# Two transformer layers on one Trainium2 core: the planner keeps the DMA queue's time, and head outputs wait in a list of their own

## The chip, the cores and the metric

The kernel runs on one core of one Trainium2 (trn2) chip. The core has five engines that run their own instruction streams and wait for one another through semaphores: PE (TensorE, matrix products; its weight loads are shown apart as PEld), ACT (ScalarE), DVE (VectorE), POOL (GpSimd) and SP (SyncE, which here only issues DMA transfers). The metric is the device time of one execution in microseconds. Times of kernels are medians of several runs; a profile shows one execution, with its own time.

## The reference

Input x is 2048 rows of 512 (bf16). Two equal layers follow each other, and both use the same weights:

```
x = x + attention(layernorm(x))     # 32 heads of 16, full softmax over all 2048 keys, then @ wo
x = x + silu(layernorm(x) @ w1) @ w2   # inner width 1792
```

The attention computes `softmax(q @ k.T / 4) @ v` for every head, without a mask. There are 32 x 2048 x 2048 exponentials in each layer.

## The kernel before

**Tiling.** The 2048 rows are cut into four chunks of 512, `c` for the keys and `qc` for the queries, `L` is the layer. Heads come in four groups `g` of eight, and each group in two halves `par` of four heads; the four heads of a half share the 128 rows of PE as four 32-row tiles. One run is (L, qc, g, par) over 16 key tiles `kt`, and in one step of a run one key tile meets 512 queries for four heads, so a run has 16 steps; there are 1024 steps in all. Layer 0's first query chunk goes over the keys in four passes and layer 1's first in two (PASSES), because its keys are only being made then.

**A step.** PE makes four score blocks (`s_ps`, three of them for ACT, and `d_ps`, L763). ACT takes the exponential of three (`p_sb`, L990, in one activation over one block and one over two). DVE and POOL make the fourth by integer arithmetic on the bits of a half-precision number: DVE writes `d_y` (L910), POOL two shifted copies `d_z` (L930), whose sum with weights approximates the exponential; the weights are in scaled copies of V, `VB`, which POOL makes from `VA` (L481). On every second step PE adds up the weighted values of two steps into `o_ps` (L787). The denominators come along as a column of ones in V.

**Everything else is background work**, put between the steps: layer norms (statistics on DVE and POOL, `xn` on DVE at L339, then a DMA transpose on SP into `xnT` or `fT`, L373), projections (`proj_k`, `proj_q`, `proj_v`, all through `mm4`, matmuls at L397), the end of a run (`group_out`: `o_ps` copied to `oT` by DVE, a DMA transpose into `ot` at L499, reciprocal `rec` at L519 and the normalised product into `attn` at L521), the output projection (`out_proj`: four DMA transposes of `attn` into the free part of `wo`, L557, then four products `y_ps` that are added to x, L545) and the feed-forward part (`ffn`: 14 products `h_ps`, tanh on ACT, `hT` on DVE, then `f_ps`). A projected q does not go where it is used at once: DVE copies it to `q` (L442; two buffers), and eight small DMA transfers on SP spread it over `QT` (L444).

**What sets the order.** The order on each engine is fixed when the program is built. Every background job is a generator, whose `yield part(...)` tells what comes next (time on PE, time on DVE, whether it holds the single bank for products, what it needs). `Background` has a queue, a side list for layer norms, and a list of `urgent` ends of runs, each with a step from which it may be taken. A small model of the engines (`Model`) keeps the clocks of PE, ACT and DVE while the program is built; a part is placed into a step when it `fits`, that is when PE would be back in time for ACT, or DVE would end before ACT. Where a step needs something that is not placed yet, `ensure` places it there, fit or not. Where PE has room that no part fills, `fill` places 3 x 4 products with a zero matrix.

**What the model before knows of transfers.** Any part on DVE that does not hold the bank sets `landed` to DVE's clock plus TRANSPOSE = 3.0 (L173), as if a transpose had been issued there; a finished layer norm keeps that number, and what needs it is placed once PE's clock has passed it. SP's own queue is not modelled. The output projection's transposes count as landed at once:

```
            nc.sync.dma_start_transpose(out=aT[:, i, :, :], in_=attn[L, qc][:, i, :])
        bg.done["aT", L, qc] = 0.0
```

The end of a run by DMA is `urgent` from five steps after the run's last one, whether its transpose has landed or not.

Of the kernel before, what the change touches and what calls it, by code (L numbers as in the profile page):

```python
# [23 lines left out]
def part(dve=0.0, pe=0.0, held=False, sums=False, need=None):  # L24

    return Part(held, pe, dve, sums, need)

class Background:

    def __init__(self):  # L30
        self.queue = deque()
        self.side = deque()
        self.urgent = deque()
        self.active = None
        self.done = {None: 0.0}
        self.model = None
# [24 lines left out]
    def advance(self, item):  # L61
        if self.model:
            self.model.charge(item[2])
        try:
            item[2] = next(item[1])
        except StopIteration:
            if item is self.active:
                self.active = None
            else:
                (self.side if self.side and item is self.side[0] else self.queue).remove(item)  # L70
                self.done[item[0]] = self.model.landed if self.model else 0.0

    def heads(self, now):
        return [self.head(now), self.prime(self.side[0]) if self.side else None]

    def fits(self, item):
        if item is None or item[2].need not in self.done:
            return False
        return self.model.fits(item[2], self.done[item[2].need])
# [11 lines left out]
class Model:  # L91
# [8 lines left out]
    FIX = 0.69  # L100
    FROM_ACT = 0.17
    FROM_DVE = 0.06
    TRANSPOSE = 3.0

    def __init__(self, slack, margin):
        self.slack, self.margin = slack, margin
        self.pe = self.act = self.dve = self.ready = self.free = 0.0
        self.s1 = self.sd = self.copied = self.landed = 0.0
        self.s2 = [0.0, 0.0]
        self.mode = None  # L110

# [25 lines left out]
    def pv(self, groups):  # L137
# [2 lines left out]
        self.pe += self.GROUP * groups  # L140
        self.summed = self.pe + self.TO_DVE

    def pe_end(self, pe, sums):
        start = max(self.pe, self.free, self.copied if sums else 0.0)
        return start + pe + self.SWITCH * (self.mode != "B")

    def fits(self, cost, landed=0.0):
        held, pe, dve, sums, _ = cost
        if landed > self.pe:
            return False  # L150
        if pe:
            end = self.pe_end(pe, sums) + self.SWITCH
            return end + self.GROUP + self.TO_ACT + self.margin <= self.act
        if dve:
            return max(self.dve, self.ready if held else 0.0) + dve <= self.act + self.slack
        return True
# [5 lines left out]
    def charge(self, cost):  # L162
        held, pe, dve, sums, _ = cost
        if pe:
            self.pe = self.pe_end(pe, sums)
            self.mode = "B"
            self.ready = self.pe + self.TO_DVE
        elif dve:
            self.dve = max(self.dve, self.ready if held else 0.0) + dve
            if held:  # L170
                self.free = self.dve + self.FROM_DVE
            else:
                self.landed = self.dve + self.TRANSPOSE  # L173
        elif held:
            self.act = max(self.act, self.ready) + self.TANH
            self.ready = self.act + self.FROM_ACT

@with_exitstack
def kernel(
# [10 lines left out]
    nc = tc.nc  # L190
# [59 lines left out]

    x1 = [x1pool.tile([P, 4, D], BF16, name=f"x1_{c}")[:] for c in range(NC)]
    x_sb = {}

    def load_x(c, src=None, parts=1):
        x_sb[c] = xpool.tile([P, 4, D], BF16, name="x", tag="x")
# [31 lines left out]
    bg = Background()  # L287
# [5 lines left out]
    attn = {}  # L293
# [58 lines left out]
    def ln_pair(c, i):  # L352

        stats[c, i] = yield from ln_stats(c, (i, i + 1))
# [11 lines left out]
    def ln_chunk(c, dst):  # L366

        for i in (0, 2):
            mv, rstd = stats.pop((c, i))
            for u in range(2):  # L370
                yield part(0.57)
                xn = ln_apply(c, i + u, mv[:, u, :], rstd[:, u, :])
                nc.sync.dma_start_transpose(out=dst[:, i + u, :, :], in_=xn[:])  # L373

    def ln_ahead(c):
        for i in (0, 2):
# [43 lines left out]
    def proj_q(L, c, g):  # L420


        yield part(need=("ln", L, c))
        q_ps = yield from mm4(
            "q_ps", lambda ct: w_qkv[:, ct, P * g : P * (g + 1)], lambda ct: xnT[L, c][:, :, ct, :]
        )
        if (L, c) == (0, 0):
            QT[g] = qpool.tile([P, 2, 512], BF16, name="QT", tag=f"QT{g}")
            for par in range(2):
                if par == 1 and g == 0:  # L430
                    nc.scalar.activation(
                        QT[g][:, par, :], q_ps, ACT.Copy, scale=masks[par][:, 0:1]
                    )
                    return
                nc.vector.tensor_scalar_mul(
                    out=QT[g][:, par, :], in0=q_ps, scalar1=masks[par][:, 0:1]
                )
                if par == 0 and g > 0:
                    yield part(0.65, held=True)
            return  # L440
        q = qpool.tile([P, 512], BF16, name="q", tag="q", bufs=2)
        nc.vector.tensor_copy(out=q[:], in_=q_ps)  # L442
        for r in range(0, P, 16):
            nc.sync.dma_start(QT[g][r : r + 16, r // 16 % 2, :], q[r : r + 16, :])  # L444

    def new_v(L, c):
        VA[L, c] = vpool.tile([P, 4, VW], BF16, name="VA", tag="VA")
# [44 lines left out]
    def by_dma(L, qc, g, par):  # L492
        return (L, qc) not in PASSES and (L, qc, g, par) != (1, NC - 1, NG - 1, 1)

    def group_out(L, qc, g, par, oT):

        if by_dma(L, qc, g, par):
            ot = opool.tile([P, 4, P], BF16, name="ot", tag="ot")
            nc.sync.dma_start_transpose(out=ot[:], in_=oT[0])  # L499
            yield part(0.25)  # L500
            att = ot[:].rearrange("p t (j s) -> p t j s", j=4)
        else:
            at_once = 4 if len(oT) <= 2 else 2
            yield part(pe=0.06 * at_once * len(oT), sums=True)
            att = bank("att").rearrange("p (t j s) -> p t j s", t=4, j=4)
            for tq in range(4):
                if tq == at_once:
                    yield part(pe=0.06 * at_once * len(oT), held=True)
                for i, o in enumerate(oT):
                    nc.tensor.matmul(  # L510
                        att[:, tq, :, :].rearrange("p j s -> p (j s)"),
                        lhsT=o[:, tq * P : (tq + 1) * P],
                        rhs=ident[:, :],
                        start=(i == 0),
                        stop=(i == len(oT) - 1),
                    )
            yield part(0.25, held=True)
        rec = small.tile([P, 4, 4, 1], FP32, name="rec", tag="rec")
        nc.vector.reciprocal(rec[:], att[:, :, :, 16:17])  # L519
        yield part(0.43, held=not by_dma(L, qc, g, par))  # L520
        nc.vector.tensor_tensor(  # L521
            out=attn[L, qc][:, :, P * g : P * (g + 1)].rearrange(
                "p t (j s) -> p t j s", s=32
            )[:, :, :, 16 * par : 16 * par + 16],
            in0=att[:, :, :, 0:DH],
            in1=rec[:].to_broadcast([P, 4, 4, DH]),
            op=ALU.mult,
        )
# [23 lines left out]
    def out_proj(L, qc):  # L552
        if (L, qc) == (0, 0):
            load_wo()
        aT = wo[0][:, CT : 2 * CT, :].rearrange("p t (c q) -> p t c q", c=CT)
        for i in range(4):
            nc.sync.dma_start_transpose(out=aT[:, i, :, :], in_=attn[L, qc][:, i, :])  # L557
        bg.done["aT", L, qc] = 0.0
        for i in range(4):
            yield from out_add(qc, i, aT[:, i, :, :])  # L560
            if i % 2:
                bg.add_side(None, ln_pair(qc, i - 1))
        bg.add_side(("fT", L, qc), ln_ffn(L, qc))
# [21 lines left out]
    class W1:  # L585
# [14 lines left out]

        def get(self, ft):
            self.load(ft + 2)
            return self.tiles.pop(ft)

    def ffn(L, c):
# [133 lines left out]
    for ts in pv_steps.values():  # L739
        t, k = ts[0]  # L740
# [148 lines left out]
    def end_run(t, key, o):  # L889

        nc.vector.tensor_copy(out=o, in_=o_tiles[key][:])  # L891
        if not final[key]:
            return
        L, qc, pi, g, par = key
        need = ("aT", *((L, qc - 1) if qc else (L - 1, NC - 1))) if (L, qc) != (0, 0) else None
        gen = end_group(L, qc, g, par)
        if by_dma(L, qc, g, par):
            bg.urgent.append((t + 5, gen, need, next(gen)))
        else:
            bg.urgent.append((t + 2, gen, need, None))  # L900

# [51 lines left out]
    with tc.manual_schedule(  # L953
# [59 lines left out]
        for t in range(1, len(steps)):  # L1013
# [5 lines left out]
            L, qc, pi, g, par, kt, j = a_blks[0]  # L1019
# [37 lines left out]
            if not busy and m.fill_fits(FILL):  # L1057
                n = fill(FILL)
                if n:
                    m.pv(n)  # L1060
        t = len(steps) + 1
# [38 lines left out]
```

## Time and profile before

| | |
|---|---|
| median of 3 runs | 1686.08 us (1683.26 to 1686.69) |
| the profiled execution | 1692.16 us, of which 1690.4 us are the span from the first instruction to the last |
| ACT busy | 1513.3 us, 90% of the span |
| PE busy | 1515.2 us, 90% |
| POOL, DVE busy | 1127.4 us, 67%; 1051.1 us, 62% |
| mean granted clock of PE | 0.950 of full |

A row of the groups reads: line, engine, operation, output <- inputs, shape, count, then busy time and the mean of one in ns, then how long the engine was idle just before them and what ended that. A row of the waits reads: who waited, for whom: total us, times, longest. A row of the stretches gives each engine's busy time in a window, with the number of its instructions that touch the window, then the granted clock of PE (PEclk, 1.00 is full), the mean share of the DMA engines and GB/s.

### The profile page before, as it was taken

The numbers are of one execution on the slowest core, as the hardware profiler recorded it, in microseconds if no ns is written. First come the engines' busy times: TensorE is split into PE (matmuls) and PEld (weight loads), VectorE is DVE, ScalarE is ACT, GpSimd is POOL, SyncE is SP. The second block draws the span as 40 slices with busy tenths as digits, with TensorE's granted clock in tenths as the row PEclk, the third lists the DMA queues.
The fourth block names the chain that finished last, engine by engine and source line by source line (L and its number), as shares of the span: only waits on it lengthen the run. The fifth ranks groups of instructions, "written<-read, shape, count | busy, mean of one in ns | idle before, by whom it ended". The sixth has DMA issues, their size and how long they took to land.

```text
span 1690.4 us, 34407 instructions
## 1 busy us (share of the span) xinstructions
PE 1515.2 (90%) x13471; PEld 468.3 (28%) x13471; DVE 1051.1 (62%) x1723; ACT 1513.3 (90%) x2169; POOL 1127.4 (67%) x1180
## 2 busy tenths in 40 slices
PE   7889997898899988999888979889889898899998
PEld 2222332232222322222222323223222232222323
DVE  4776765666666656666666647666557655576544
ACT  4888997998899988999889959899889998899992
POOL 3677866676776767767766757767667676676750
PEclk7898998999999989999999989999899999999999
DMA  3101012101111011201021010120102101121101
GB/s 118 27 13 26 4 26 54 35 17 44 39 39 28 29 28 42 44 23 34 19 51 38 8 32 11 47 48 13 33 20 48 35 20 30 39 42 26 29 14 47
DMA packets 154770, 55.84 MB, mean 33 GB/s; under 512 B 134896, under 2 KB 154096, under 8 KB 154608
## 3 DMA queue, kind: packets, MB, share of 16 engines
q1 hardware_dynamic: 154608, 53.65, 13.5%
q8 instruction: 105, 1.72, 0.5%
q14 instruction: 57, 0.47, 0.1%
HBM read 28.57 MB, written 4.19 MB: 19 GB/s over the span
## 4 chain that ended last, share of the span: by engine, by line
ACT 66%; PE 21%; DVE 4%; DMA 3%; issue 3%; SPq 2%; POOL 0%; DVEq 0%; ACTq 0%
ACT p_sb L990 62%; PE o_ps L787 7%; PE s_ps L763 6%; ACT t_sb L566 3%; SPq L444 2%; PE k_ps L397 2%; PE v_ps L397 1%; DVE d_y L910 1%; PE y_ps L397 1%; PE q_ps L397 1%; DMA wo<-attn 1%; PE d_ps L763 1%; DMA xnT<-xn 1%; DMA ot<-oT 1%; PE h_ps L397 1%
## 5 line engine op out<-in xcount | busy, mean ns | idle before, releaser
L990 ACT ACTIVATE p_sb<-s_ps 128x512 bf16<-128x512 f32 x2042 | 1489.5, 1075 | 130.0 <-PE d_ps L763 79.1
L910 DVE TENSOR_SCALAR d_y<-d_ps 128x512 uint16<-128x512 f32 x1020 | 703.8, 690 | 489.8 <-PE d_ps L763 441.7
L763 PE MATMUL s_ps<-QT,KT 32*128 32x512 bf16 x3076 | 630.0, 391 | 65.8 <-ACT p_sb L990 53.3
L763 PE MATMUL d_ps<-QT,KT 32*128 32x512 bf16 x1020 | 402.4, 394 | 20.7 <-DVE d_y L910 10.9
L763 PEld LDWEIGHTS <-KT 32*128 32x128 bf16 x4096 | 184.5, 91 | 679.6 <-issue 628.0
L787 PE MATMUL o_ps<-p_sb,VA 128*32 128x512 bf16 x3063 | 323.9, 398 | 10.0 <-DVE oA L891 2.0
L787 PE MATMUL o_ps<-d_y,VA 128*32 128x512 f16 x1020 | 161.1, 393 | 0.0
L787 PEld LDWEIGHTS <-VA 128*32 128x32 bf16 x4096 | 88.2, 96 | 149.1 <-issue 106.9
L787 PE MATMUL o_ps<-w_qkv,zero 128*32 128x512 bf16 x1512 | 112.0, 404 | 0.0
L626 PE MATMUL f_ps<-w_sb,hT 128*128 128x512 bf16 x392 | 103.7, 381 | 0.0
L787 PEld LDWEIGHTS <-VB 128*32 128x32 f16 x2040 | 80.3, 99 | 62.5 <-issue 6.5
L566 ACT ACTIVATE t_sb<-h_ps 128x512 f32<-128x512 f32 x98 | 92.1, 940 | 1.0 <-PE h_ps L397 1.0
L569 DVE SCALAR_TENSOR_TENSOR hT<-t_sb,h_ps 128x512 bf16<-128x512 f32 x98 | 67.4, 688 | 23.9 <-ACT t_sb L566 23.9
L397 PE MATMUL y_ps<-wo 128*128 128x512 bf16 x120 | 40.0, 461 | 29.5 <-DMA wo<-attn 29.1
L397 PE MATMUL k_ps<-xnT,w_qkv 128*128 128x512 bf16 x128 | 40.4, 441 | 25.8 <-DMA xnT<-xn 24.8
L891 DVE CAST oT<-o_ps 128x512 bf16<-128x512 f32 x64 | 43.6, 681 | 7.7 <-PE o_ps L787 7.7
L787 PEld LDWEIGHTS <-zero 128*32 128x32 bf16 x1512 | 29.5, 98 | 58.5 <-issue 46.1
L397 PE MATMUL v_ps<-w_qkv,xnT 128*128 128x512 bf16 x128 | 39.2, 424 | 6.6 <-DVE VA L462 6.4
L329 DVE BATCH_NORM_STATS2 st<-x 128x6 f32<-128x512 bf16 x64 | 43.7, 682 | 1.9 <-DMA x<-in_A_x_dram 1.9
L418 DVE CAST KT<-k_ps 128x512 bf16<-128x512 f32 x32 | 22.0, 688 | 36.7 <-PE k_ps L397 36.5
L626 PEld LDWEIGHTS <-hT 128*128 128x128 bf16 x392 | 29.6, 97 | 45.6 <-issue 23.9
L397 PEld LDWEIGHTS <-w_qkv 128*128 128x128 bf16 x256 | 20.6, 102 | 64.5 <-issue 46.8
(2333 smaller groups left out, 2083.0 us busy)
## 6 DMA issues: line engine op xcount, KB each, us to landing
wo<-in_A_wo_dram SPq DMA_DIRECT2D x8, 512.0 KB, 3.7
x<-in_A_x_dram SPq DMA_DIRECT2D x7, 512.0 KB, 4.3
QT<-q SPq DMA_DIRECT2D x224, 16.0 KB, 1.8
out_dram<-x SPq DMA_DIRECT2D x16, 128.0 KB, 1.8
w_sb<-in_B_w_dram SPq DMA_DIRECT2D x1, 1792.0 KB, 13.2
w_qkv<-in_A_wqkv_dram SPq DMA_DIRECT2D x3, 512.0 KB, 6.6
ot<-oT SPq DMA_TRANSPOSE x47, 2.3
x<-in_A_x_dram SPq DMA_DIRECT2D x2, 256.0 KB, 2.9
```

The lines of the kernel that those rows point to most:

```text
L329: nc.vector.bn_stats(st[:], x_sb[c][:, i, :])
L397: nc.tensor.matmul(ps.rearrange("p (t q) -> p t q", q=P) if len(r.shape) == 3 else ps, lhsT=lhs(ct), rhs=r, start=(ct == 0), stop=(ct == C ...
L418: nc.vector.tensor_copy(out=KT[L, c][:, g, :], in_=k_ps)
L444: nc.sync.dma_start(QT[g][r : r + 16, r // 16 % 2, :], q[r : r + 16, :])
L566: nc.scalar.activation(t_sb, h_ps, ACT.Tanh, scale=0.5)
L569: nc.vector.scalar_tensor_tensor(out=hT[:, ft, :], in0=t_sb, scalar=1.0, in1=h_ps, op0=ALU.add, op1=ALU.mult)
L626: nc.tensor.matmul(y_ps, lhsT=hT[:, ft, tq * P : (tq + 1) * P], rhs=w2_sb[:, ft, :], start=(ft == 0), stop=(ft == FT - 1),)
L763: nc.tensor.matmul(out, lhsT=KT[L, kt // 4][r, g, (kt % 4) * P : (kt % 4 + 1) * P], rhs=QT[g][r, par, :], start=True, stop=True,)
L787: nc.tensor.matmul(o_tiles[key][32 * j : 32 * j + 32, :], lhsT=lhsT, rhs=rhs, start=(o_count[key][j] == 0), stop=stop,)
L891: nc.vector.tensor_copy(out=o, in_=o_tiles[key][:])
L910: nc.vector.tensor_scalar(out=pr["y"][:, len(pr["ds"]), :], in0=s_ps[:], scalar1=float(1024 * SCALE * math.log2(math.e)), scalar2=float(10 ...
L990: nc.scalar.activation(p_sb, s_ps, ACT.Exp, bias=-SHIFT * math.log(2.0) + math.log(EXP_SUM), scale=float(SCALE),)
```

## The change

SP gets a clock in the model (`sp`). A DMA transpose goes through a helper that adds 1.27 us to it, from DVE's clock plus 0.1 at the earliest, and sets `landed` 1.7 us behind it; the eight transfers of a q add 8 x 0.64, a load of a w1 tile 0.64. What needs transposed data is now placed once the clock of its first engine has passed that landing: the output projection waits for its four transposes (a `part` of no cost), and the end of a run for its one. These ends have left `urgent` for a list of their own, `outs`, which is asked first at every step. The loads of x, of wo and of the first two w1 tiles, and the stores, add nothing to the clock.

```diff
     def heads(self, now):
-        return [self.head(now), self.prime(self.side[0]) if self.side else None]
+        return [
+            self.outs[0] if self.outs else None,
+            self.head(now),
+            self.prime(self.side[0]) if self.side else None,
+        ]
...
-    TRANSPOSE = 3.0
+    TRANSPOSE = 1.27
+    TRANSPOSED = 1.7
+    DMA = 0.64
...
+    def transpose(self):
+        self.sp = max(self.sp, self.dve + 0.1) + self.TRANSPOSE
+        self.landed = self.sp + self.TRANSPOSED
+
+    def dma(self, n):
+        self.sp = max(self.sp, self.dve + 0.1) + n * self.DMA
+
...
     def fits(self, cost, landed=0.0):
         held, pe, dve, sums, _ = cost
-        if landed > self.pe:
+        if landed > (self.pe if pe else self.dve):
             return False
...
             if held:
                 self.free = self.dve + self.FROM_DVE
-            else:
-                self.landed = self.dve + self.TRANSPOSE
...
+    def transpose(out, in_):
+        nc.sync.dma_start_transpose(out=out, in_=in_)
+        if bg.model:
+            bg.model.transpose()
+
...
         for r in range(0, P, 16):
             nc.sync.dma_start(QT[g][r : r + 16, r // 16 % 2, :], q[r : r + 16, :])
+        if bg.model:
+            bg.model.dma(8)
...
             ot = opool.tile([P, 4, P], BF16, name="ot", tag="ot")
-            nc.sync.dma_start_transpose(out=ot[:], in_=oT[0])
-            yield part(0.25)
+            transpose(ot[:], oT[0])
+            bg.done["ot", L, qc, g, par] = bg.model.landed
+            yield part(0.25, need=("ot", L, qc, g, par))
...
         for i in range(4):
-            nc.sync.dma_start_transpose(out=aT[:, i, :, :], in_=attn[L, qc][:, i, :])
-        bg.done["aT", L, qc] = 0.0
+            transpose(aT[:, i, :, :], attn[L, qc][:, i, :])
+        bg.done["aT", L, qc] = bg.model.landed
+        yield part(need=("aT", L, qc))
...
         if by_dma(L, qc, g, par):
-            bg.urgent.append((t + 5, gen, need, next(gen)))
+            assert need in bg.done
+            bg.outs.append(["out", gen, next(gen)])
         else:
             bg.urgent.append((t + 2, gen, need, None))
```

No instruction is added, and the only ones that go are fillers: 126 groups of 12 products with zeros are placed before, 118 now. All else is moved. Three places on DVE show it; a row's number of L910 products (`d_y`, one in a step) is a ruler of steps.

The first is the output projection of layer 0's second query chunk: `rec` and `attn` are the last end of a run, right after which SP issues the four transposes, and `x<-x,y_ps` adds the first of the four products that need them (`q` and `KT` are a projected q and k). Before:

```order
L442 CAST q<-q_ps 128x512
L910 TENSOR_SCALAR d_y<-d_ps 128x512 x3
L519 RECIPROCAL rec<-ot 128x16
L521 TENSOR_TENSOR attn<-ot,rec 128x4x4x16
L910 TENSOR_SCALAR d_y<-d_ps 128x512
L545 TENSOR_TENSOR x<-x,y_ps 128x512
```

The same place now:

```order
L460 CAST q<-q_ps 128x512
L935 TENSOR_SCALAR d_y<-d_ps 128x512 x2
L540 RECIPROCAL rec<-ot 128x16
L542 TENSOR_TENSOR attn<-ot,rec 128x4x4x16
L935 TENSOR_SCALAR d_y<-d_ps 128x512
L436 CAST KT<-k_ps 128x512
L935 TENSOR_SCALAR d_y<-d_ps 128x512 x8
L566 TENSOR_TENSOR x<-x,y_ps 128x512
```

One step lay between `attn` and the first addition, and nine do now.

The second is the layer norm of layer 1's first chunk (`xn`, the last three of four rows of tiles, each transposed by SP) and the first projection from it (`KT`). Before:

```order
L339 TENSOR_SCALAR xn<-x,mv,rstd 128x512
L910 TENSOR_SCALAR d_y<-d_ps 128x512
L339 TENSOR_SCALAR xn<-x,mv,rstd 128x512
L910 TENSOR_SCALAR d_y<-d_ps 128x512
L339 TENSOR_SCALAR xn<-x,mv,rstd 128x512
L910 TENSOR_SCALAR d_y<-d_ps 128x512 x5
L418 CAST KT<-k_ps 128x512
```

The same place now, with the end of a run (`oT`, `rec`, `attn`) inside it:

```order
L357 TENSOR_SCALAR xn<-x,mv,rstd 128x512
L935 TENSOR_SCALAR d_y<-d_ps 128x512
L357 TENSOR_SCALAR xn<-x,mv,rstd 128x512
L935 TENSOR_SCALAR d_y<-d_ps 128x512
L357 TENSOR_SCALAR xn<-x,mv,rstd 128x512
L935 TENSOR_SCALAR d_y<-d_ps 128x512 x4
L915 CAST oT<-o_ps 128x512
L935 TENSOR_SCALAR d_y<-d_ps 128x512 x4
L540 RECIPROCAL rec<-ot 128x16
L542 TENSOR_TENSOR attn<-ot,rec 128x4x4x16
L935 TENSOR_SCALAR d_y<-d_ps 128x512
L436 CAST KT<-k_ps 128x512
```

Five steps lay between the last `xn` and the first k, and nine do now.

The third is early in layer 0: the values of the third chunk (`VA<-v_ps`, four copies, after the last of which POOL scales them into `VB`) beside the ends of the second pass's runs (`oB<-o_ps`). The excerpts start at the same `oB`, the last but one of that pass. Before:

```order
L891 CAST oB<-o_ps 128x512
L910 TENSOR_SCALAR d_y<-d_ps 128x512
L462 CAST VA<-v_ps 128x32x16
L910 TENSOR_SCALAR d_y<-d_ps 128x512
L462 CAST VA<-v_ps 128x32x16
L910 TENSOR_SCALAR d_y<-d_ps 128x512
L339 TENSOR_SCALAR xn<-x,mv,rstd 128x512
L910 TENSOR_SCALAR d_y<-d_ps 128x512
L891 CAST oB<-o_ps 128x512
L910 TENSOR_SCALAR d_y<-d_ps 128x512
L462 CAST VA<-v_ps 128x32x16
L418 CAST KT<-k_ps 128x512
```

The same place now:

```order
L915 CAST oB<-o_ps 128x512
L935 TENSOR_SCALAR d_y<-d_ps 128x512
L482 CAST VA<-v_ps 128x32x16
L935 TENSOR_SCALAR d_y<-d_ps 128x512
L436 CAST KT<-k_ps 128x512
L935 TENSOR_SCALAR d_y<-d_ps 128x512
L357 TENSOR_SCALAR xn<-x,mv,rstd 128x512
```

The last copy of the chunk's values came five steps after this `oB`, and comes one step after it now.

More of the change, by code (lines that the diff above doesn't have):

```diff
@@ L32, in __init__ @@
         self.side = deque()
+        self.outs = deque()
         self.urgent = deque()
@@ L69, in advance @@
             else:
-                (self.side if self.side and item is self.side[0] else self.queue).remove(item)
+                home = [q for q in (self.outs, self.side, self.queue) if item in q][0]
+                home.remove(item)
                 self.done[item[0]] = self.model.landed if self.model else 0.0
     def heads(self, now):
-        return [self.head(now), self.prime(self.side[0]) if self.side else None]
+        return [
[3 more added lines that the diff above has]
+        ]
     def fits(self, item):
@@ L107, in __init__ @@
         self.pe = self.act = self.dve = self.ready = self.free = 0.0
-        self.s1 = self.sd = self.copied = self.landed = 0.0
+        self.s1 = self.sd = self.copied = self.sp = self.landed = 0.0
         self.s2 = [0.0, 0.0]
@@ L372, in ln_chunk @@
                 xn = ln_apply(c, i + u, mv[:, u, :], rstd[:, u, :])
-                nc.sync.dma_start_transpose(out=dst[:, i + u, :, :], in_=xn[:])
+                transpose(dst[:, i + u, :, :], xn[:])
     def ln_ahead(c):
@@ L602, in get @@
             self.load(ft + 2)
+            if bg.model:
+                bg.model.dma(1)
             return self.tiles.pop(ft)
```

## The prediction

> **What bounds the kernel now.** The page comes first, then the chain of waits, then the stretches.
>
> ```profile
> PE 1515.2 (90%) x13471; PEld 468.3 (28%) x13471; DVE 1051.1 (62%) x1723; ACT 1513.3 (90%) x2169; POOL 1127.4 (67%) x1180
> L990 ACT ACTIVATE p_sb<-s_ps 128x512 bf16<-128x512 f32 x2042 | 1489.5, 1075 | 130.0 <-PE d_ps L763 79.1
> ```
>
> ```profile
> 536.05 49.73 ACT p_sb L990 x71
> ```
>
> ACT's exponentials set the pace: where nothing disturbs them the chain of waits runs through ACT alone, 49.73 us for 71 activations, two of them a step, so 1.40 us a step. PE is as busy over the span, but off the chain there. What can be won is ACT's idle time, 130.0 us ahead of the exponentials, and only where it is not ACT's own work that comes late. The list of waits says whose it is:
>
> ```profile
> ACT p_sb L990 <- PE d_ps L763: 79.1, 48, 7.5
> ACT p_sb L990 <- PE s_ps L763: 38.2, 16, 11.9
> PE y_ps L397 <- DMA wo<-attn: 29.1, 7, 4.6
> PE k_ps L397 <- DMA xnT<-xn: 24.8, 4, 9.2
> DVE rec L519 <- DMA ot<-oT: 7.3, 4, 3.2
> PE d_ps L763 <- DMA QT<-q: 6.4, 1, 6.4
> PE o_ps L787 <- POOL VB L481: 2.7, 2, 2.3
> DVE q L442 <- DMA QT<-q: 4.6, 2, 2.6
> ```
>
> ACT waits for scores, and the scores stand behind something in PE's or DVE's order that waits for a transfer: 29.1 + 24.8 us on PE for transposes. One of the seven output projections, in time order:
>
> ```profile
> 449.97 6.10 SPq L557 DMA_TRANSPOSE wo<-attn  x4
> 452.38 1.89 PE L397 MATMUL y_ps<-wo 128*128 128x512 bf16 x4 [4.63 <-DMA wo<-attn]
> 454.87 1.51 ACT L990 ACTIVATE p_sb<-s_ps 128x512 bf16<-128x512 f32 x2 [5.24 <-PE d_ps L763]
> ```
>
> SP issues four transposes, PE stands 4.63 us at the first product until the first has landed, and ACT stands 5.24. What each such place costs is read from the stretches as width less ACT's busy time:
>
> ```profile
> core 0: us, PE busy (x) PEld busy (x) DVE busy (x) ACT busy (x) POOL busy (x), PEclk, DMA share, GB/s
> 138.00:152.00 14.00, 10.77 (x70) 2.39 (x72) 6.56 (x12) 7.55 (x12) 8.21 (x15) 0.76 0.14 28
> 240.00:252.00 12.00, 10.00 (x81) 3.07 (x80) 6.79 (x13) 9.65 (x14) 6.64 (x7) 0.86 0.34 87
> 270.00:290.00 20.00, 13.56 (x128) 3.58 (x124) 8.66 (x17) 11.41 (x16) 8.90 (x9) 0.74 0.33 74
> 290.00:300.00 10.00, 7.85 (x65) 2.13 (x58) 5.38 (x9) 8.56 (x14) 5.24 (x6) 0.83 0.48 65
> 410.00:422.00 12.00, 6.78 (x44) 1.71 (x44) 3.65 (x6) 5.18 (x9) 3.98 (x6) 0.72 0.18 36
> 448.00:461.00 13.00, 8.62 (x54) 2.12 (x54) 6.23 (x11) 6.90 (x11) 4.51 (x6) 0.74 0.53 108
> 461.00:611.00 150.00, 141.10 (x1304) 43.36 (x1302) 100.29 (x165) 149.96 (x219) 111.16 (x111) 1.00 0.13 31
> 611.00:624.00 13.00, 8.14 (x50) 1.96 (x50) 4.42 (x8) 5.95 (x9) 4.55 (x6) 0.61 0.20 41
> 649.00:662.00 13.00, 8.79 (x53) 2.13 (x54) 6.02 (x11) 6.68 (x11) 4.31 (x5) 0.74 0.42 107
> 812.00:824.00 12.00, 7.43 (x54) 1.98 (x54) 4.86 (x8) 6.51 (x11) 5.17 (x8) 0.72 0.21 44
> 849.00:862.00 13.00, 9.17 (x68) 2.33 (x69) 6.38 (x12) 7.30 (x12) 5.03 (x5) 0.74 0.42 106
> 980.00:1018.00 38.00, 25.77 (x207) 7.26 (x206) 17.66 (x30) 18.64 (x27) 17.46 (x26) 0.82 0.12 32
> 1060.00:1072.00 12.00, 7.37 (x60) 1.95 (x52) 4.39 (x8) 6.70 (x11) 4.19 (x4) 0.72 0.41 107
> 1215.00:1224.00 9.00, 6.34 (x65) 1.48 (x64) 4.05 (x7) 5.88 (x9) 4.29 (x5) 0.81 0.01 1
> 1261.00:1273.00 12.00, 8.03 (x50) 1.95 (x50) 5.62 (x10) 6.29 (x10) 3.98 (x5) 0.72 0.44 112
> 1414.00:1422.00 8.00, 5.65 (x61) 1.34 (x60) 3.79 (x7) 4.62 (x7) 4.19 (x4) 0.79 0.05 12
> 1460.00:1470.00 10.00, 6.41 (x44) 1.63 (x44) 3.96 (x8) 4.61 (x7) 3.01 (x3) 0.66 0.48 117
> ```
>
> The stretch 461 to 611, with no such place, keeps ACT busy 149.96 of 150 us: a wait that goes is a gain in full, as long as the work behind it finds other room.
>
> **The change, part by part.**
>
> The output projection (L557, `aT`). Its seven places are the stretches from 240, 448, 649, 849, 1060, 1261 and 1460: 2.35 + 6.10 + 6.32 + 5.70 + 5.30 + 5.71 + 5.39 = 36.87 us. Now nine steps lie between `attn` and the first addition, 12.6 us, and the product takes 1.89 of them, which leaves some 10. The transposes need
>
> ```profile
> DMA to landing us min/median/max: 2.3/2.4/4.0
> ```
>
> and 6.10 us for all four issues, so the last lands at most 3.9 + 4.0 = 7.9 us after the first issue. The term is taken whole, 36.9; its lower bound, with 1.6 us (4.0 less 2.4) left at each place, is 25.7. Meanwhile the queue behind `wo` stands, and PE gets scores, values and fillers. The four products, at most 1.89 us each, go to steps that were filled with zeros (eight groups of 12 fillers fewer), so they cost nothing there; in steps without such room each would cost its own length.
>
> The layer norms (L373). Stretches from 410, 611 and 812: 6.82 + 7.05 + 5.49 = 19.36 us; from 290, where `h_ps` waits for `fT`, 1.44. Nine steps instead of five, 12.6 us, follow the last `xn`. What made these late is SP, which had 24 transfers of q ahead. At another place such a series stands alone:
>
> ```profile
> 1196.06 16.08 SPq L444 DMA_DIRECT2D QT<-q  x24
> ...
> QT<-q SPq DMA_DIRECT2D x224, 16.0 KB, 1.8
> ```
>
> 0.67 us each, and a median of 1.8 from issue to landing. From the second of the three q casts on, 15 steps, 21 us, now pass until the first k is copied; 16 transfers (10.7), four transposes (5.2) and a landing (2.4) need 18.3, and the product before that copy needs 1.9. This is the tightest place: taken whole at 20.8, at least 14.4 with 1.6 left at each of four.
>
> Ends of runs (L499). In the stretches from 1215 and 1414 `rec` stood behind 24 transfers of q: 3.12 + 3.38 = 6.50 us. They wait in their list now, and `attn` is not needed until the chunk ends: 6.5, at least 3.3 if half stays. The stretches just ahead of these lose time to the q cast, which waits for a free `q` buffer (4.6 us on DVE); those casts stay where they were and nothing is won there.
>
> Values (L481). In 138 to 152 PE waits for `VB`: 6.45 us. The last `VA` copy comes four steps earlier, 5.6 us against a wait of 2.3, because the earlier layer norms are let through sooner: 6.45, at least 3.
>
> What stays. The stretch 980 to 1018 (19.36 us): `ensure` forces the last layer norm and the first k of chunk 3 into one step; the change leaves the same pieces of the feed-forward part and the same layer norm in that step. From 270 to 290 (8.59) `d_ps` waits for `QT`: the three q casts now come two steps apart, and the first transfer of the third starts 16 x 0.67 = 10.7 us after the first cast and takes 1.8 to land, with five to six steps (7 to 8.4 us) to hide it: a wait of 4 to 5.5 in place of 6.4. I take 1 us; bounds -2 to 3, for in its new place it stands behind more transfers. The start and the tail keep their order.
>
> Where ACT waits, its two activations also overlap less: 1.51 us for a step's two (454.87) against 1.40 in the chain. With three to four such steps at each of 13 places that adds about 5 us.
>
> Sum: 36.9 + 20.8 + 6.5 + 6.5 + 1 + 5 = 76.7. The profiled execution took 1692.16 us (span 1690.4 and 1.76 around it), so 1615.5. It lies 6.1 us above the median of the runs, 1686.08, from which the same sum gives 1609.4; I take 1610. With the lower bounds the sum is 25.7 + 14.4 + 3.3 + 3 - 2 + 0 = 44, which is 1642.
>
> After a wait PE also runs slowly for a while:
>
> ```profile
> 244.84 1.04 PE L397 MATMUL y_ps<-wo 128*128 128x512 bf16 x4 [1.90 <-DMA wo<-attn]
> ...
> 244.00:246.00 2.00, 1.16 (x8) 0.41 (x8) 0.08 (x1) 0.83 (x1) 0.61 (x1) 1.00 0.62 140
> 246.00:250.00 4.00, 4.00 (x28) 0.91 (x24) 2.08 (x4) 3.02 (x4) 2.09 (x2) 0.57 0.15 33
> ```
>
> Behind a wait of 1.90 us the granted clock falls from 1.00 to a mean of 0.57, and the slow steps there are already in its 2.35 us. [...]
>
> **The rivals.**
>
> *Landings later than the planner counts (partial).* SP also carries loads of x, wo and w1 and stores that add nothing to its clock, and the planner counts 1.27 + 1.7 = 2.97 us for a transpose where up to 4.0 was measured. For it: that maximum, and the tightest sum above, which has 21 - 18.3 - 1.9 = 0.8 us of room. Against it: some 10 us less 7.9 at `aT`. Price at 13 places: 1.6 us and one slow step,
>
> ```profile
> 283.44 1.51 ACT L990 ACTIVATE p_sb<-s_ps 128x512 bf16<-128x512 f32 x2 [7.47 <-PE d_ps L763]
> 285.39 1.51 ACT L990 ACTIVATE p_sb<-s_ps 128x512 bf16<-128x512 f32 x2 [0.43 <-PE d_ps L763]
> ```
>
> 1.95 less 1.40 = 0.55: 28 us given back, 1638.
>
> [...]
>
> *The order changes and the waits do not.* If PE were the true limit, the products would only be late elsewhere and the time would stay at 1684. For it: PE is busy 90%. Against: ACT at 149.96 of 150.
>
> *More than the sum.* The layer norms of the start also come earlier; another 10 us, 1598.
>
> **How the numbers follow.** The forecast, 1610 with its own range 1602 to 1624, has 0.76; partial 0.14; slower 0.04; unchanged 0.02; more 0.04. The range 1599 to 1642 takes in all lower bounds at once and leaves out the slower and unchanged cases, and the ends of partial and more. Below 0.2% (3.4 us) a measurement of this kernel cannot tell a change from none: faster 0.94, same 0.02, slower 0.04.
>
> **What would show it.** Right: the waits of `y_ps` for `wo<-attn` (29.1) and of `rec` for `ot` (7.3) near zero; `k_ps` for `xnT` left with the one of about 9 us that `ensure` forces; PEclk 1.00 where the seven projections stand; ACT's idle time ahead of `p_sb` near 60. Wrong: `y_ps` waits of 1 to 2 us at every place (partial); PEclk near 0.5 in the steps between `attn` and `y_ps`, or ACT waiting for `s_ps` with no transfer behind it (slower, or PE the limit); a longer stall at `ensure` or at `QT`.

## The result: 1636.4 us, and where the missing third of the gain stayed

The changed kernel takes 1636.43 us (median of 4 runs, 1630.01 to 1638.98) against 1684.67 of the kernel before beside it: a ratio of 0.971 (95% interval 0.968 to 0.974), 48 us less. The forecast was 1610. The profiled execution took 1638.98 us, its span 1637.2, against 1692.16 and 1690.4: 53.2 us less, of the 76.7 in the sum.

The page of the changed kernel, the lines that answer to those shown of before (engines; the costliest group):

```profile
PE 1499.6 (92%) x13375; PEld 465.8 (28%) x13375; DVE 1067.6 (65%) x1723; ACT 1509.8 (92%) x2169; POOL 1122.5 (69%) x1180
L1015 ACT ACTIVATE p_sb<-s_ps 128x512 bf16<-128x512 f32 x2042 | 1483.6, 1087 | 81.6 <-PE s_ps L787 36.0
```

ACT's idle time ahead of the exponentials fell from 130.0 to 81.6; the forecast had said near 60. From its list of waits (waiter, what it waited for: us in total, times, longest):

```profile
DVE xn L357 <- DMA xnT<-xn: 20.1, 4, 6.4
PE k_ps L415 <- DMA xnT<-xn: 9.8, 2, 9.2
PE d_ps L787 <- DMA QT<-q: 6.2, 1, 6.2
DVE xn L357 <- DMA fT<-xn: 2.9, 1, 2.9
DVE rec L540 <- DMA ot<-oT: 2.2, 4, 0.9
```

The 29.1 us of `y_ps` for `wo<-attn` are gone, `rec` for `ot` went from 7.3 to 2.2, and of `k_ps` for `xnT` only the forced 9.2 is left, with 0.6 elsewhere. All this is as forecast. The first row is what the forecast did not have: VectorE now waits 20.1 us at the writes of `xn`. The stretches of the changed kernel: three output projections, from the four transposes to the last of the four products, then three layer norms and the forced layer norm.

```profile
core 0: us, PE busy (x) PEld busy (x) DVE busy (x) ACT busy (x) POOL busy (x), PEclk, DMA share, GB/s
436.00:458.00 22.00, 21.59 (x204) 6.55 (x200) 15.60 (x26) 22.00 (x33) 17.56 (x17) 1.00 0.33 68
631.00:653.00 22.00, 21.59 (x212) 6.52 (x208) 16.27 (x27) 22.00 (x33) 17.09 (x18) 1.00 0.28 68
828.00:850.00 22.00, 21.74 (x208) 6.71 (x208) 14.73 (x25) 22.00 (x33) 18.02 (x19) 1.00 0.13 27
396.00:408.00 12.00, 7.32 (x53) 1.45 (x52) 4.38 (x7) 6.17 (x9) 5.09 (x5) 0.64 0.30 59
591.00:603.00 12.00, 6.67 (x57) 1.49 (x60) 4.28 (x7) 5.83 (x9) 4.81 (x5) 0.72 0.24 48
787.00:799.00 12.00, 6.62 (x49) 1.34 (x48) 4.37 (x7) 5.50 (x9) 4.39 (x5) 0.56 0.24 49
952.00:990.00 38.00, 25.90 (x185) 6.94 (x183) 15.85 (x27) 16.19 (x23) 15.09 (x24) 0.73 0.13 32
```

Where a projection stands, ACT is busy all 22 us and the granted clock is 1.00 (so it is at the other four). Where a layer norm stands, ACT is idle 5.83, 6.17 and 6.50 of 12 us, as much as the 6.82, 7.05 and 5.49 before. What happens there, in time order (start, length, idle time in brackets):

```profile
391.71 4.96 SPq L462 DMA_DIRECT2D QT<-q  x8
396.77 5.14 SPq L268 DMA_TRANSPOSE xnT<-xn  x4
...
392.30 0.40 DVE L357 TENSOR_SCALAR xn<-x,mv,rstd 128x512 bf16<-128x512 bf16 x1
393.10 0.69 DVE L935 TENSOR_SCALAR d_y<-d_ps 128x512 uint16<-128x512 f32 x1 [0.40 <-PE d_ps L787]
399.31 0.41 DVE L357 TENSOR_SCALAR xn<-x,mv,rstd 128x512 bf16<-128x512 bf16 x1 [5.51 <-DMA xnT<-xn]
...
400.37 0.58 PE L787 MATMUL d_ps<-QT,KT 32*128 32x512 bf16 x1 [4.53 <-DVE d_y L935]
...
402.97 1.51 ACT L1015 ACTIVATE p_sb<-s_ps 128x512 bf16<-128x512 f32 x2 [5.23 <-PE s_ps L787]
```

A layer norm writes four `xn` into a ring of three (`xnpool`, `bufs=3`). The third is written at 392.30. The fourth needs the first buffer, which comes free when its transpose has landed, and SP issues that transpose only at 396.77, behind transfers of q. The chain of waits names it:

```profile
396.77 2.44 DMA xnT<-xn
```

It lands at 399.21, and the fourth `xn` starts at 399.31. VectorE stands 5.51 us; the next `d_y` stands behind it, PE behind `d_y` (4.53), ACT behind PE (5.23). The wait that the planner took from PE came back on VectorE, from the same transposes behind the same transfers.

Both traces cut into the same stretches of steps (a step's two exponentials carry its number, so the same step can be timed in both) give the balance: the seven projections, twelve steps each, -38.8 us; the layer norms of the later chunks +1.1 and the `fT` and `QT` stretch -1.2; the ends of runs -9.8; the wait for `VB` -6.8; the start -4.2; the forced layer norm +2.5; all other steps +4.1, in small pieces. Together that is -53.2, apart from rounding. Where a stretch is cut moves a figure by about 1 us.

### The profile page after: what moved, and what is told of

Its sections match the earlier page's. It is cut to its first block, busy times and chain, and to the rows that moved or that the text cites. A ratio compares the mean times of both kernels' runs of the same rounds, so it can differ in the third digit from the quotient of the medians.

```text
span 1637.2 us, 34184 instructions
## 1 busy us (share of the span) xinstructions
PE 1499.6 (92%) x13375; PEld 465.8 (28%) x13375; DVE 1067.6 (65%) x1723; ACT 1509.8 (92%) x2169; POOL 1122.5 (69%) x1180
## 4 chain that ended last, share of the span: by engine, by line
ACT 73%; PE 15%; DVE 4%; issue 3%; SPq 2%; DMA 2%; POOL 0%; DVEq 0%; ACTq 0%
ACT p_sb L1015 70%; PE o_ps L811 5%; PE s_ps L787 4%; ACT t_sb L588 3%; SPq L462 2%; DVE d_y L935 1%; PE v_ps L415 1%; PE h_ps L415 1%; DMA xnT<-xn 1%; PE d_ps L787 1%; PE q_ps L415 1%; PE f_ps L709 1%; PE y_ps L415 0%; PE k_ps L415 0%; DVE st L347 0%
## 5 line engine op out<-in xcount | busy, mean ns | idle before, releaser
L1015 ACT ACTIVATE p_sb<-s_ps 128x512 bf16<-128x512 f32 x2042 | 1483.6, 1087 | 81.6 <-PE s_ps L787 36.0
L787 PE MATMUL d_ps<-QT,KT 32*128 32x512 bf16 x1020 | 398.6, 391 | 31.8 <-DVE d_y L935 21.9
L811 PE MATMUL o_ps<-w_qkv,zero 128*32 128x512 bf16 x1416 | 104.7, 404 | 0.0
L357 DVE TENSOR_SCALAR xn<-x,mv,rstd 128x512 bf16<-128x512 bf16 x64 | 34.2, 542 | 24.9 <-DMA xnT<-xn 20.1
L415 PE MATMUL k_ps<-xnT,w_qkv 128*128 128x512 bf16 x128 | 37.0, 403 | 10.8 <-DMA xnT<-xn 9.8
L415 PE MATMUL v_ps<-w_qkv,xnT 128*128 128x512 bf16 x128 | 38.8, 419 | 6.7 <-DVE VA L482 5.9
L542 DVE TENSOR_TENSOR attn<-ot,rec 128x256 bf16<-128x256 bf16 x47 | 42.3, 899 | 1.6
L415 PE MATMUL q_ps<-xnT,w_qkv 128*128 128x512 bf16 x128 | 33.8, 381 | 0.4 <-DVE KT L436 0.4
```

What stands on the lines that cost most here:

```text
L357: nc.vector.tensor_scalar(out=xn[:], in0=x_sb[c][:, i, :], scalar1=mv[:, 0:1], scalar2=rstd, op0=ALU.subtract, op1=ALU.mult,)
L415: nc.tensor.matmul(ps.rearrange("p (t q) -> p t q", q=P) if len(r.shape) == 3 else ps, lhsT=lhs(ct), rhs=r, start=(ct == 0), stop=(ct == C ...
L542: nc.vector.tensor_tensor(out=attn[L, qc][:, :, P * g : P * (g + 1)].rearrange("p t (j s) -> p t j s", s=32)[:, :, :, 16 * par : 16 * par ...
L787: nc.tensor.matmul(out, lhsT=KT[L, kt // 4][r, g, (kt % 4) * P : (kt % 4 + 1) * P], rhs=QT[g][r, par, :], start=True, stop=True,)
L811: nc.tensor.matmul(o_tiles[key][32 * j : 32 * j + 32, :], lhsT=lhsT, rhs=rhs, start=(o_count[key][j] == 0), stop=stop,)
L1015: nc.scalar.activation(p_sb, s_ps, ACT.Exp, bias=-SHIFT * math.log(2.0) + math.log(EXP_SUM), scale=float(SCALE),)
```

## Experiments

All runs are compared with the kernel before on the same chip (medians 1687 to 1689 there, 1684.67 beside the changed kernel). A difference of two medians can be off by some 3 us for that: the 8 us of run 4 are 6 by the ratios.

**Run 1: four buffers in place of three.**

```diff
-    xnpool = ctx.enter_context(tc.tile_pool(name="xnpool", bufs=3))
+    xnpool = ctx.enter_context(tc.tile_pool(name="xnpool", bufs=4))
```

> The changed kernel with a ring of four xn buffers instead of three; every engine's list of instructions stays the same, so only waits can move. Theory 'the layer norms' wait has moved' (PE no longer waits for xnT, but the fourth xn now waits on VectorE for the first buffer, which comes free only when a transpose behind 24 transfers of q has landed): the 20.1 + 2.9 us that VectorE waits for xnT<-xn and fT<-xn go, and with them ScalarE's idle stretches of 5.23, 5.73, 6.07 and 2.85 us, 19.9 in all: 1636 - 20 = 1616 (1613 to 1621). Rival 'landings later than the planner counts': the k products then wait for the landed xnT in the place of xn, 4 to 5.5 us at each of three places, and the time stays at 1632 to 1638.

1610.77 us, ratio 0.954 (0.952 to 0.956): 26 us less than the changed kernel. From the page and the waits:

```profile
L1015 ACT ACTIVATE p_sb<-s_ps 128x512 bf16<-128x512 f32 x2042 | 1483.9, 1094 | 53.0 <-PE s_ps L787 26.9
```

```profile
PE k_ps L415 <- DMA xnT<-xn: 10.6, 3, 9.2
```

No row of `xn` waiting for a transfer is left, no new wait of `k_ps` came (9.2 of its 10.6 are the forced one), and ACT's idle time fell by 28.6. By steps, the three layer norms won 21.0 us and the one of `fT` 3.8: 24.8, a little above the expected 20. So a landing time that the planner counts too short is not the cause: once the buffer is there, the products find their data landed.

**Run 2: the same buffer in the kernel before.** The same edit.

> The kernel before with a ring of four xn buffers; the same lists of instructions. Theory 'the wait has moved': in the kernel before PE meets the missing xnT itself (24.8 us of k_ps waits, three of some 5 us), and VectorE waits only 1.8 us for xn, so the buffer alone is worth no more than 2 us: 1682 to 1686. If buffers of xn were short in themselves, whatever the placement, it would gain about as much as in the changed kernel: near 1665.

1686.38 us, ratio 1.000 (0.999 to 1.001). There the waits stay where they were:

```profile
PE y_ps L397 <- DMA wo<-attn: 30.3, 7, 5.0
PE k_ps L397 <- DMA xnT<-xn: 24.4, 5, 9.2
```

The buffer is worth nothing without the new placement, and the placement nothing at the layer norms without the buffer.

**Run 3: a landing counted 1.6 us later.**

```diff
-    TRANSPOSED = 1.7
+    TRANSPOSED = 3.3
```

> The changed kernel with the planner's landing time of a transpose set to 3.3 us instead of 1.7, so work on transposed data is placed about one step later. Rival 'landings later than the planner counts': leftovers of 1 to 2 us at 13 places go, some 20 to 28 us are won, 1608 to 1618. Theory 'the wait has moved': no consumer waits for a landing now, but for the one product that is forced; the time stays within 6 us of the changed kernel, 1630 to 1642, and VectorE's wait for xn stays at 15 us or more.

1642.17 us, ratio 0.973 (0.971 to 0.974), nothing won. VectorE's waits for `xn` stay:

```profile
DVE xn L357 <- DMA xnT<-xn: 13.8, 4, 5.6
DVE xn L357 <- DMA fT<-xn: 8.1, 2, 4.5
```

**Run 4: the products of the output projection let go at once.**

```diff
-        bg.done["aT", L, qc] = bg.model.landed
-        yield part(need=("aT", L, qc))
+        bg.done["aT", L, qc] = 0.0
```

> The changed kernel with the output projections let go at once again (the landing of aT counted as time zero, the separate wait left out), all else as changed. The forecast's first term: the waits of y_ps for wo<-attn come back with about 29 us on PE, 37 us of ScalarE's idle time (up to 42 with the slower steps behind them): 1636 + 37 to 42 = 1673 to 1678. If the products' place were worth less than the term, because the queue of transfers or the list of outs brings the gain: below 1655.

1644.39 us, ratio 0.974 (0.973 to 0.976): 8 us lost, not 37 to 42. A miss. The wait did come back, and others shrank:

```profile
PE y_ps L415 <- DMA wo<-attn: 26.0, 7, 5.3
DVE xn L357 <- DMA xnT<-xn: 13.3, 3, 6.2
DVE xn L357 <- DMA fT<-xn: 7.2, 1, 7.2
```

By steps the seven places lose 32.8 us, close to the term of the sum. But what stands behind the products in the background list is then placed earlier (the stall of the layer norms, for one, by 8 to 17 steps): the layer norms with `fT` lose 9.3 us less, the forced one 7.0 less (3.3 for 9.2 in `k_ps`), the ends of runs 2.2, other steps some 6.

**Run 5: runs 1 and 4 together.**

> Four xn buffers, and the output projections let go at once again (the edit that cost 8 us in the changed kernel, though the waits of y_ps for wo<-attn came back with 26 us there). Theory 'holding the products pushes the layer norms into the three buffers' (the price at the products is some 35 us, and most of it is given back because the background work, no longer held, comes earlier and meets shorter waits for xn and at the forced layer norm): with the fourth buffer there is little left to give back, and the edit costs 20 to 30 us: 1611 + 20 to 30 = 1631 to 1641. Rival 'the products' place was never worth more than some 8 us, because what waits there only moves the waits of others': again 5 to 10 us, 1616 to 1621.

1627.68 us, ratio 0.964 (0.962 to 0.967): with four buffers the holding is worth 17 us in the medians, between the two expectations. The places lose 34.3 us (`y_ps` waits 26.2); 4.8 come back at the forced layer norm, 4.9 at the ends of runs, 1.4 at `QT` and `fT`, the rest in small pieces, and 20.8 are left by steps. So some 25 us were given back in run 4 and 14 to 17 here (by steps, by the medians): 8 to 11 of them belonged to the three buffers. The rest looks like a price of holding itself, as all background work behind the products starts later; shown is that only at the forced layer norm, where there is a due time.

**Run 6: run 1, and q groups made in the order of need.**

```diff
-        self.queue.insert(int(begun) if first else len(self.queue), [label, gen, None])
+        at = int(begun)
+        while first and at < len(self.queue) and self.queue[at][0][0] == "q":
+            at += 1
+        self.queue.insert(at if first else len(self.queue), [label, gen, None])
```

> Four xn buffers, and projections of q that are put at the head of the list go behind those already there, so a chunk's q groups are made in the order in which they are needed; group 1 of chunk 1 is then cast at step 137 in place of 155 and the first output projection moves from step 141 to 154. The one wait of d_ps for QT<-q (5.7 to 6.2 us, ScalarE idle 6.4) goes: 1611 - 6 = 1605 (1602 to 1608). If the wait were the queue's and not the order's, it would come back at another group: 1609 to 1613.

1605.94 us, ratio 0.952 (0.949 to 0.955). The wait of `d_ps` for `QT<-q` has left the list, and steps 154 to 162 won 6.7 us; some of it went in small pieces elsewhere.

**Run 7: head outputs back among the urgent pieces, three buffers.**

```diff
-            bg.outs.append(["out", gen, next(gen)])
+            bg.urgent.append((t + 5, gen, need, next(gen)))
```

> The changed kernel with the head outputs put back among the urgent pieces, due five steps after the end of their group; all else as changed. The forecast's third term: rec waits for ot again, 6.5 us by the forecast, 10 by what the two traces differ at these places: 1643 to 1647. Rival: the list of its own brings nothing, the earlier gain at these places is the queue clock's, which spaces the casts of q: 1633 to 1639.

1624.71 us, ratio 0.963 (0.961 to 0.965): 12 us faster, where both expectations had it the same or slower. From its waits:

```profile
PE h_ps L415 <- DMA w<-in_B_w_dram: 9.9, 2, 9.3
PE d_ps L787 <- DMA QT<-q: 8.8, 1, 8.8
DVE xn L357 <- DMA xnT<-xn: 6.1, 3, 2.2
```

`rec` waits for no `ot`, so it is not the list that keeps the pieces back until they have landed. And VectorE's waits for `xn` are 6.1 in place of 23.0. SP's queue at the same layer norm shows why. In the changed kernel all 24 transfers of q stand ahead of the first transpose:

```profile
380.75 15.93 SPq L462 DMA_DIRECT2D QT<-q  x24
396.77 5.14 SPq L268 DMA_TRANSPOSE xnT<-xn  x4
```

In run 7 the transposes come between them:

```profile
385.20 5.78 SPq L462 DMA_DIRECT2D QT<-q  x8
391.08 1.21 SPq L268 DMA_TRANSPOSE xnT<-xn  x1
392.39 4.96 SPq L462 DMA_DIRECT2D QT<-q  x8
```

At the other two layer norms 16 transfers stand ahead of the transposes there, in place of 24. An urgent piece, once begun, is the only one that the main list offers until it has landed; that this is what holds the casts of q back is read from the code, not shown by itself. Two long waits are new.

**Run 8: the layer norms' old landing time.**

```diff
                 transpose(dst[:, i + u, :, :], xn[:])
+                if bg.model:
+                    bg.model.landed = bg.model.dve + 3.0
```

> The changed kernel with three buffers in which the layer norms alone get their old landing time back, 3.0 us behind VectorE's clock whatever stands in the queue; output projections, outs and all else as changed. Forecast's second term: 20.8 us are lost, 1636 + 21 = 1657 (at least 1650). Theory 'the wait has moved': with three buffers this part of the change brought nothing, the wait goes back from VectorE's xn to PE's k_ps and v_ps, and since products then come some 5 steps earlier a little may even be won at the forced layer norm: 1628 to 1642.

1638.80 us, ratio 0.971 (0.969 to 0.973), within 2.4 us of the changed kernel: the 20.8 us that the forecast gave this part are not there to lose. `k_ps` has taken back a part of the wait and `xn` kept the rest:

```profile
PE k_ps L417 <- DMA xnT<-xn: 18.3, 5, 9.1
DVE xn L357 <- DMA xnT<-xn: 15.9, 4, 4.8
```

**Run 9: run 6, and each product held for its own transpose alone.**

```diff
             transpose(aT[:, i, :, :], attn[L, qc][:, i, :])
+            bg.done["aT", L, qc, i] = bg.model.landed
         bg.done["aT", L, qc] = bg.model.landed
-        yield part(need=("aT", L, qc))
         for i in range(4):
+            yield part(need=("aT", L, qc, i))
```

> Four xn buffers and q groups in order, as in the run at 1606, and each of the four products of an output projection is held only for its own transpose, not for the last of the four; the first product then stands some three steps (4 us) earlier, and chunk 3's feed-forward part ends ahead of the forced layer norm (step 600 of 605). Theory 'holding costs what it delays': the stall at the forced layer norm (ScalarE 11.9 + 1.3) shrinks by 3 to 6 us, as it shrank by 7 where the products were not held at all, and no wait of y_ps for wo<-attn comes back: 1606 - 5 = 1601 (1597 to 1604). Rival 'transposes land later than the planner counts': the nearer placement brings back 1 to 2 us at each of seven places, 1606 + 5 to 10 = 1611 to 1616.

1600.80 us (median of 5, 1599.10 to 1606.11), ratio 0.949 (0.946 to 0.951): the fastest median of all, 36 us under the changed kernel. The interval overlaps that of run 6, so the 5 us between them are not settled; the two profiled executions differ the other way (1606.11 against 1604.79). Both mechanisms show in its waits:

```profile
PE k_ps L418 <- DMA xnT<-xn: 7.4, 3, 6.2
PE y_ps L418 <- DMA wo<-attn: 3.8, 3, 1.9
```

The forced wait went from 9.2 to 6.2, and at two of seven projections a wait came back, of 1.90 and 1.71 us: there the first transpose had not landed when its product's turn came, though the planner counts 2.97 us from its issue.

**Run 10: runs 1 and 7 together.**

> Four xn buffers and the head outputs back among the urgent pieces. With three buffers that edit won 12 us where a loss had been expected, and VectorE's waits for xn fell from 23.0 to 6.1. Theory 'an urgent piece that waits holds the main list back, which spaces the casts of q and spares the three buffers': with four buffers nothing is left to spare, and the time is that of four buffers alone, 1611 (1606 to 1616). Rival 'the list of its own costs 12 us whatever the buffers': 1599 (1596 to 1602).

1624.67 us, ratio 0.962 (0.959 to 0.965): 14 us slower than run 1. The rival falls, and so does "nothing is left", for the urgent order has its own price, the two long waits of run 7:

```profile
PE h_ps L415 <- DMA w<-in_B_w_dram: 9.5, 2, 8.9
PE d_ps L787 <- DMA QT<-q: 8.7, 1, 8.7
```

One of them in time order:

```profile
472.23 5.11 SPq L462 DMA_DIRECT2D QT<-q  x8
477.39 0.58 SPq L278 DMA_DIRECT2D x<-in_A_x_dram  x1
478.33 12.48 SPq L618 DMA_DIRECT2D w<-in_B_w_dram  x6
...
482.54 1.89 PE L415 MATMUL h_ps<-fT,w 128*128 128x512 bf16 x4 [8.93 <-DMA w<-in_B_w_dram]
```

A cast of q has moved ahead of the feed-forward part, whose first weights now stand behind eight transfers. So the list of its own is worth 14 us with four buffers and costs 12 with three, where its order puts the casts of q in one block ahead of the layer norm.

**Run 11: a head output placed as soon as its transpose is issued.**

```diff
-            yield part(0.25, need=("ot", L, qc, g, par))
+            yield part(0.25)
```

> The changed kernel, three buffers, list of outs kept, but a head output is placed as soon as its transpose is issued, not once it has landed. Theory 'what won the 10 us at the ends of runs is the landing, not the list': the waits of rec for ot come back at 20 us or more, since every one of the 47 pieces may now be early by up to 2.3 us, and the time rises to 1645 to 1690. Rival 'the list and the queue clock alone win it': 1630 to 1640.

1757.97 us, ratio 1.041 (1.038 to 1.044), beyond what was expected. From its waits:

```profile
DVE rec L540 <- DMA ot<-oT: 128.2, 47, 7.2
```

All 47 pieces wait, 2.7 us each on average, and what stands behind them on VectorE waits with them: PE's `d_ps` waits 111.1 us for `d_y`, in place of 21.9 in the changed kernel. With run 7 this shows for the third term that the landing keeps `rec` from waiting, whichever list the piece is in. Run 11 also goes without the five steps of delay that the kernel before had, so it does not tell what the new order would have won with that delay alone.

## Why the forecast was right on the sign and 26 us off

The measured 1636 lies outside the forecast's own range, 1602 to 1624. That the wide range, 1599 to 1642, holds it is luck: that range adds up every lower bound, and none of these stood for a wait that goes to VectorE.

**What bounds the kernel** held: nearly all of the gain came out of ACT's idle time (48.4 us of idle time against 53.2 of span). The rest is the term of 5 us for activations that overlap less beside a wait: the busy time of the exponentials fell from 1489.5 to 1483.6 us.

**The output projections, 36.9 us: right at their places** (38.8 won by steps, with the slower steps in them; the wait gone, clock 1.00). That the products "cost nothing" where they went held too. What the term left out is the price of the delay for the work behind them, which runs 4 and 5 put at some 25 us with three buffers (32.8 - 8) and 14 to 17 with four (34.3 - 20.8 by steps, 34.3 - 17 with the medians).

**The layer norms, 20.8 us: the step that failed.** "What made these late is SP, which had 24 transfers of q ahead" was right, and the room counted up to the copy of the first k sufficed (run 1). But the sum looked only at who uses a transpose's result. It did not ask who waits for its source to be read: the fourth write of `xn`, in a ring of three. With `fT` and `QT` a gain of 21.8 was forecast for these stretches; by steps they won 0.1 (+1.1 and -1.2). Run 8 says the same from the other side, and run 1 brings the term with the buffer. The "tightest place" was sought on PE; it was on VectorE.

**The ends of runs, 6.5: 9.8**, the cause right in part: as far as runs 7 and 11 show, the landing did it, not the list. **Values, 6.45: 6.8. QT, 1:** the wait went from 6.4 to 6.2; its cause is the order in which the groups are cast (run 6). **The start** was taken as unchanged and won 4.2; in run 2, with the old order, it differs by 2.9 as well. **The forced layer norm** was to stay at 19.36 and is 21.8 by width less busy time (38.00 - 16.19). The 4.1 us in small pieces were not followed further.

**The rivals.** "Landings later than the planner counts" named 1638, and the time is 1636, yet its mechanism is not what happened: no `y_ps` wait of 1 to 2 us stands at the projections, and counting later won nothing (run 3). Only where the products were moved nearer did such waits return, at two places (run 9). The slower case, a PEclk near 0.5 between `attn` and `y_ps`, did not come: the clock is 1.00 at the projections. "The order changes and the waits do not" came true for the layer norms and for `QT`, though not for its reason, PE as the limit: it should have been asked of each term, not of the whole.

## What to carry to other kernels

A transfer has two ends to wait for: when its result has landed (here `k_ps` waited 24.8 us for `xnT` in the kernel before), and when its source may be written again (`xn` waited 20.1 us in the changed one). Before a producer is let run ahead of a late queue, count the buffers of its ring; here one buffer of 128x512 was worth 26 us with the new order and nothing without. And price a hold by all that is queued behind it up to the next due time, not only by the wait that it removes.

## What the chip showed that was not expected

The clock does not follow the length of a wait. In the kernel before, a wait of 1.90 us at a projection was followed by four microseconds at a mean clock of 0.57. In run 9 a wait of the same length at the same kind of place was not (first the timeline, then the stretches, whose seventh figure behind the stretch's name is the granted clock):

```profile
254.89 1.04 PE L418 MATMUL y_ps<-wo 128*128 128x512 bf16 x4 [1.90 <-DMA wo<-attn]
```

```profile
253.40:256.80 3.40, 1.91 (x20) 0.64 (x20) 1.24 (x3) 1.95 (x4) 1.18 (x2) 1.00 0.95 199
256.80:260.20 3.40, 3.40 (x34) 0.94 (x28) 2.66 (x5) 3.40 (x6) 2.16 (x3) 1.00 0.47 88
```

And in the changed kernel two shorter ones were; the clock fell during the second:

```profile
1172.99 0.37 PE L787 MATMUL d_ps<-QT,KT 32*128 32x512 bf16 x1 [1.11 <-DVE d_y L935]
1174.22 0.58 PE L787 MATMUL d_ps<-QT,KT 32*128 32x512 bf16 x1 [0.64 <-DVE d_y L935]
```

```profile
1170.70:1174.10 3.40, 1.77 (x19) 0.35 (x12) 1.92 (x4) 3.40 (x6) 1.20 (x2) 1.00 0.10 24
1174.10:1177.50 3.40, 3.26 (x25) 0.70 (x28) 1.84 (x4) 1.69 (x4) 2.82 (x4) 0.50 0.12 29
```

In the traces of the kernel before and of the changed kernel any two changes of the clock lie a whole multiple of 3.41 us apart, and their stretches here are cut on that raster. Of the raster stretch ahead PE was busy 1.56 us in the kernel before (243.00 to 246.40) and 1.77 in the changed one, and the clock fell; in run 9 it was busy 1.91 us of the 3.40 from 253.40, and the clock stayed. The busy time alone does not settle it: in the changed kernel the clock also fell at 184.30, behind a stretch with PE busy 2.75 us.

So slow steps came behind one wait of 1.90 us and not behind the other, and the 0.55 us that the prediction put on each leftover wait was too sure.
